# A raw weight tile of 6,208 instead of 6,152 bytes in a kernel bound by its matmuls

## The chip, the cores and the metric

The kernel runs on one core of a Trainium2 chip. The metric is the device time of one execution in microseconds (us); shorter is better. The engines are named as the profile names them: PE is TensorE (PEld its weight loads), DVE is VectorE, ACT is ScalarE, POOL is GpSimd, SP is SyncE, which issues most of the DMAs.

## The reference

Three stages, one behind the other, all in float32: attention with a soft cap on the scores, a gated MLP with an RMS norm ahead of it, and a second MLP with a PReLU.

```python
scores = cap * np.tanh(scale * (q @ k.T) / cap)        # 2 x 12 heads, 448 x 448, head_dim 64
attn   = softmax(scores); x = attn @ v                 # -> x: 896 tokens x 768
xn = x / rms(x) * rms_g
x  = (silu(xn @ w_gate) * (xn @ w_val)) @ w_out        # 768 -> 1536 -> 768
h  = x @ w_in                                          # 768 -> 2048
g  = np.maximum(h, 0) + alpha * np.minimum(h, 0)
out = g @ w_out2                                       # 2048 -> 768
```

## The kernel before

**Stages.** The attention works on 12 pairs of heads (6 pairs for each of 2 batches). All that follows, called the MLP part here, is a list of "slots": each slot is one product of 18 matmuls, and the work of the other engines is hung on slot numbers. The slots are the layers "g" (gate and value, 6 groups of 7 products), "o" (first output projection, 22 slots), "z" (4 groups of 7 products), and the last layer "c" and "f" (16 and 14 slots). The products of seven per group are a Strassen scheme (names P1 to P7, S1 to S4, T1 to T4).

**One matmul.** In the MLP part every matmul takes 128x128 weights (the stationary operand, 512 bytes in each partition) and 128x448 of activations (the moving operand, 1,792 bytes in each partition). Both are split in a high and a low half in the type fp32r, and one product is three sums of matmuls, high by high, low by high, high by low: 3 x 6 = 18 matmuls. Each matmul loads its own weights. The matmuls stand in lines 395 and 408 (layers g and z), 749 (layer o) and 775 (layers c and f). Five products have one of their matmuls cut in two (384 and 64 columns).

**Where the weights come from.** A DMA on SP's queue brings a unit of weights into a tile `raw` (line 101 and 102, three buffers, 8 bytes for each weight, landing two bytes behind the tile's start). ACT casts a part of it into `top` (line 113), DVE joins both into the float32 tile `wt` (line 118), DVE or POOL forms sums of such tiles (line 126), ACT rounds them into `wh` (line 133), and DVE subtracts to get `wl` (line 139). `wh` and `wl` are the weights of the matmuls. Two units of layer o, ("p", 0, 0) and ("p", 0, 1), are an exception: their halves are kept in tiles that otherwise hold activations (`w_kept`; the profile shows these weights as `xx` and `ks` in line 749). They serve the products c11 and c12. The products c21 and c22 of the same layer read the same activations as c11 and c12, with weights that lie in `wh` and `wl` as all others do.

**Addresses.** Tiles lie one behind the other in each partition of SBUF, pool by pool, each rounded up to 32 bytes. Constants, `wh` and `wl` lie ahead of `raw`; everything else lies behind it. The matmuls of the MLP part read slices at multiples of 512 bytes from the start of a weight tile and of 1,792 = 28 x 64 bytes from the start of an activation tile, so each operand has its tile's address modulo 64. The sums of the tile sizes give these starts:

| tile | start before | modulo 64 | start after | modulo 64 |
|---|---|---|---|---|
| `wh` (4 buffers), `wl` (4 buffers) | 8,480 to 29,984 | 32 | the same | 32 |
| `raw`, three buffers | 33,056; 39,232; 45,408 | 32; 0; 32 | 33,056; 39,264; 45,472 | 32; 32; 32 |
| `wt`, 10 buffers | from 51,584 | 0 | from 51,680 | 32 |
| activations of the MLP part, and the kept weights in them | from 82,304 | 0 | from 82,400 | 32 |
| attention: `hi`, `lo`, `vt`, `pt`, `ones`, `half`, `sel_t`, `r2` | from 150,496 | 32 | from 150,592 | 0 |

So before, a matmul of the MLP part has its weights at 32 and its moving operand at 0 modulo 64, but the matmuls of c11 and c12 have both at 0, and those of the attention both at 32.

Of the kernel before, what the change touches and what calls it, by code (L numbers as in the profile page):

```python
# [11 lines left out]
U16 = mybir.dt.uint16  # L12
# [5 lines left out]
P = 128  # L18
# [24 lines left out]
WT, WH, RAW = 10, 4, 3  # L43
# [14 lines left out]
def attn_moe_kernel(ctx: ExitStack, tc: tile.TileContext, units, qk_in, v, sel, w, gvec, alpha, out):  # L58
    nc = tc.nc
    const = ctx.enter_context(tc.tile_pool(name="const", bufs=1))  # L60
    wpool = ctx.enter_context(tc.tile_pool(name="w", bufs=1))
# [29 lines left out]
    UW = UK * P  # L91
    tops = [const.tile([P, UW], U32, name=f"top{i}") for i in range(2)]
    raw_t, f_t, h_t, l_t = {}, {}, {}, {}
# [4 lines left out]

    def w_load(u):
        i, n = units[u]  # L100
        raw_t[u] = wpool.tile([P, 4 * UW + 4], U16, tag="raw", name="raw", bufs=RAW)
        nc.sync.dma_start(out=raw_t[u][:, 1:4 * n + 1], in_=w[i][:, :n].bitcast(U16))

    def f_tile():
# [41 lines left out]
    def w_next(u):  # L146
        i = conv_seq.index(u) + RAW
        if i < len(conv_seq):
            w_load(conv_seq[i])
# [21 lines left out]
    hi, lo, raw, vt = {}, {}, {}, {}  # L171
# [242 lines left out]
    with tc.manual_schedule():  # L414
# [59 lines left out]
        for u in conv[:RAW]:  # L474
            z(0, w_load, u)
# [870 lines left out]
```

## Time and profile before

| | |
|---|---|
| time, median of 3 runs | 559.37 us (558.91 to 559.59) |
| the profiled execution's own time | 558.61 us |
| its span, from first to last instruction | 556.8 us |
| PE busy | 551.4 us, 99% |
| DVE, ACT, POOL busy | 446.9, 371.1, 97.7 us |
| granted TensorE clock | 1.00 of full speed |

The profiled execution is 1.8 us longer than its span and 0.76 us shorter than the median. A busy PE means that some matmul is in flight; since a matmul overlaps the next one, the time that one costs in a row of them is the distance from start to start, not its duration.

### The profile page before, as it was taken

The numbers are of one execution on the slowest core, as the hardware profiler recorded it, in microseconds if no ns is written. First come the engines' busy times: TensorE is split into PE (matmuls) and PEld (weight loads), VectorE is DVE, ScalarE is ACT, GpSimd is POOL, SyncE is SP. The second block draws the span as 40 slices with busy tenths as digits, with TensorE's granted clock in tenths as the row PEclk, the third lists the DMA queues.
The fourth block names the chain that finished last, engine by engine and source line by source line (L and its number), as shares of the span: only waits on it lengthen the run. The fifth ranks groups of instructions, "written<-read, shape, count | busy, mean of one in ns | idle before, by whom it ended". The sixth has DMA issues, their size and how long they took to land.

```text
span 556.8 us, 7691 instructions
## 1 busy us (share of the span) xinstructions
PE 551.4 (99%) x3061; PEld 461.0 (83%) x3061; DVE 446.9 (80%) x511; ACT 371.1 (67%) x433; POOL 97.7 (18%) x54
## 2 busy tenths in 40 slices
PE   8999999999999999999999999999999999999997
PEld 5544544799999999999999999999999999999996
DVE  4797888898998767878888798969866898999142
ACT  7989999568675455567755564787967996467110
POOL 0035762300254321010000048002111000000000
PEclk9999999999999999999999999999999999999999
DMA  7855420400434514065600662005512266013022
GB/s 255 281 182 189 145 76 4 171 1 1 167 117 154 171 74 169 13 214 181 213 4 1 227 236 104 1 0 171 186 42 85 87 226 227 0 58 114 0 100 99
DMA packets 17316, 66.09 MB, mean 119 GB/s; under 512 B 3584, under 2 KB 5504, under 8 KB 17280
## 3 DMA queue, kind: packets, MB, share of 16 engines
q1 hardware_dynamic: 16746, 65.08, 34.0%
q8 instruction: 24, 0.39, 0.3%
q10 hardware_dynamic: 390, 0.39, 0.2%
q0 software_dynamic: 144, 0.13, 0.1%
q14 instruction: 12, 0.10, 0.1%
HBM read 62.66 MB, written 2.75 MB: 117 GB/s over the span
## 4 chain that ended last, share of the span: by engine, by line
PE 97%; ACT 1%; DVE 1%; issue 0%; DVEq 0%
PE s L395 19%; PE x L395 13%; PE m L395 13%; PE s L775 9%; PE s L749 8%; PE x L775 7%; PE oo L236 6%; PE s L207 5%; PE x L749 4%; PE m L775 4%; PE rps L249 3%; PE m L749 2%; PE s L408 1%; PE x L408 1%; PE m L408 1%; ACT pt L221 1%
## 5 line engine op out<-in xcount | busy, mean ns | idle before, releaser
L133 ACT CAST wh<-wt 128x768 fp32r<-128x768 f32 x105 | 87.2, 833 | 68.2 <-PE s L775 24.6
L139 DVE TENSOR_TENSOR wl<-wt,wh 128x768 fp32r<-128x768 f32 x108 | 115.3, 1069 | 14.7 <-ACT wh L133 14.5
L126 POOL TENSOR_TENSOR wt<-wt 128x768 f32<-128x768 f32 x33 | 74.0, 2251 | 271.0 <-DVE wt L118 98.4
L113 ACT CAST top<-raw 128x768 f16<-128x768 bf16 x64 | 68.9, 1079 | 25.8 <-DVE wt L118 11.5
L118 DVE SCALAR_TENSOR_TENSOR wt<-raw,top 128x768 uint32<-128x768 uint32 x68 | 70.5, 1037 | 0.9 <-ACT top L113 0.9
L395 PE MATMUL s<-xx,wh 128*128 128x448 f32 x264 | 64.3, 368 | 0.0
L395 PEld LDWEIGHTS s<-xx,wh 128*128 128x128 f32 x264 | 49.5, 188 | 5.4 <-issue 0.7
L395 PE MATMUL x<-xx,wh 128*128 128x448 f32 x204 | 50.5, 369 | 0.0
L395 PE MATMUL m<-xx,wh 128*128 128x448 f32 x204 | 50.2, 368 | 0.0
L619 DVE TENSOR_TENSOR xx<-b,xx 128x896 fp32r<-128x896 f32 (+1 forms) x40 | 47.1, 1187 | 0.6 <-ACT xx L632 0.6
L216 ACT ACTIVATE pt<-s,cinv 128x896 f32<-128x896 f32 (+1 forms) x48 | 41.1, 911 | 5.6 <-PE s L207 5.2
L395 PEld LDWEIGHTS x<-xx,wh 128*128 128x128 f32 x204 | 38.2, 188 | 4.0 <-issue 0.4
L395 PEld LDWEIGHTS m<-xx,wh 128*128 128x128 f32 x204 | 38.3, 188 | 3.6
L775 PE MATMUL s<-xx,wh 128*128 128x448 f32 x132 | 40.7, 368 | 0.0
L236 PE MATMUL oo<-pt,vt 128*32 128x448 f32 x384 | 38.5, 540 | 0.4 <-ACT pt L221 0.3
L221 ACT ACTIVATE pt<-pt,cap_t 128x3136 f32<-128x3136 f32 (+2 forms) x13 | 35.3, 2713 | 0.4
L395 PE MATMUL s<-xx,wl 128*128 128x448 f32 x132 | 34.2, 367 | 0.0
L775 PE MATMUL x<-xx,wh 128*128 128x448 f32 x104 | 31.7, 367 | 0.0
L236 PEld LDWEIGHTS oo<-pt,vt 128*32 128x32 f32 x384 | 12.2, 110 | 23.6 <-issue 21.4
L749 PE MATMUL s<-xx,wh 128*128 128x448 f32 x96 | 27.5, 368 | 0.0
L775 PEld LDWEIGHTS s<-xx,wh 128*128 128x128 f32 x132 | 24.8, 188 | 2.3
L395 PEld LDWEIGHTS s<-xx,wl 128*128 128x128 f32 x132 | 24.8, 188 | 2.3
(223 smaller groups left out, 1119.5 us busy)
## 6 DMA issues: line engine op xcount, KB each, us to landing
raw<-w_in SPq DMA_DIRECT2D x68, 768.0 KB
rw<-qk_in SPq DMA_DIRECT2D x11, 480.0 KB
vt<-v_in SPq DMA_DIRECT2D x12, 256.0 KB
out<-b SPq DMA_DIRECT2D x2, 448.0 KB
out<-b SPq DMA_DIRECT2D x2, 224.0 KB
out<-e SPq DMA_DIRECT2D x1, 448.0 KB
out<-c SPq DMA_DIRECT2D x2, 224.0 KB
gt<-us SPq DMA_DIRECT2D x23, 3.5 KB
```

The costliest lines, as they stand in the source:

```text
L113: copy(top_of[u].bitcast(F16)[:, 1::2], raw_t[u].bitcast(BF16)[:, 4:4 * n + 4:4])
L118: nc.vector.scalar_tensor_tensor(out=f_t[u].bitcast(U32), in0=raw_t.pop(u).bitcast(U32)[:, 1:2 * n + 1:2], scalar=13, in1=top_of.pop(u), o ...
L126: add(out=t, in0=f_t[a], in1=f_t[b], op=op)
L133: copy(h_t[u], f_t[u].rearrange("p (k m) -> p k m", m=P))
L139: nc.vector.tensor_tensor(out=l_t[u], in0=f_t[u].rearrange("p (k m) -> p k m", m=P), in1=h_t[u], op=ALU.subtract)
L216: nc.scalar.activation(out=t[:, 2 * g:2 * g + w], in_=st.pop((i, g))[:, :w, :S], func=AF.Tanh, scale=cinv)
L221: nc.scalar.activation(out=t[:, done:to], in_=t[:, done:to], func=AF.Exp, scale=cap_t)
L236: nc.tensor.matmul(oo[i][q * Q:q * Q + Q, :S], vv[:, n, q % 2 * Q:q % 2 * Q + Q], t[:, min(n, TILES - 1), :], start=c == 0, stop=c == TG, ...
L395: nc.tensor.matmul(ps[:, r, c0:c1], lhs, rhs[:, c0:c1], start=first and n == 0, stop=n == len(mm) - 1, skip_group_check=True,)
L619: nc.vector.tensor_tensor(out=out, in0=a, in1=b, op=op)
L749: nc.tensor.matmul(dst[m], wt[:, kk * MB + m, :], x, start=first and u == 0 and kk == 0 and n == 0, stop=u == 1 and kk == 1 and n == 2, sk ...
L775: nc.tensor.matmul(dst[m], wt[:, kk * MB + m, :], x, start=start and ks + kk == 0 and i == 0, stop=fin and last and kk == 1 and i == 2, sk ...
```

## The change: 56 bytes more in each raw tile

The row of `raw` in the tile pool grows from 3,076 to 3,104 elements of two bytes. Nothing is written to or read from the added bytes. With the rounding to 32 bytes each of the three buffers takes 32 bytes more, so that all that lies behind `raw` moves up by 96 bytes, and its address modulo 64 by 32. The instructions and their order on every engine, the queues and the waits are the same.

```diff
     def w_load(u):
         i, n = units[u]
-        raw_t[u] = wpool.tile([P, 4 * UW + 4], U16, tag="raw", name="raw", bufs=RAW)
+        raw_t[u] = wpool.tile([P, 4 * UW + 32], U16, tag="raw", name="raw", bufs=RAW)
         nc.sync.dma_start(out=raw_t[u][:, 1:4 * n + 1], in_=w[i][:, :n].bitcast(U16))
```

## Rows read from the trace of the kernel before

**Rows 1.** The page, busy time: us (share of span) and instructions.

```profile
PE 551.4 (99%) x3061; PEld 461.0 (83%) x3061; DVE 446.9 (80%) x511; ACT 371.1 (67%) x433; POOL 97.7 (18%) x54
```

**Rows 2.** The waits of PE: engine, tile, line, cause: us, times, longest.

```profile
PE warm L419 <- DVE ones L416: 1.1, 1, 1.1
PE oo L236 <- ACT pt L221: 0.3, 1, 0.3
PE s L207 <- DVE eps_t L457: 0.2, 1, 0.2
```

**Rows 3.** The chain that ended last, in order of time: start us, us, what.

```profile
331.42 7.39 PE s L749 x36
...
342.50 3.70 PE m L395 x18
346.20 14.78 PE s L395 x72
360.98 3.70 PE x L395 x18
```

**Rows 4.** The timeline of PE around c11 and c12: start us, us, what.

```profile
264.90 0.57 PE L749 MATMUL s<-xx,wh 128*128 128x448 f32 x2
...
272.30 3.81 PE L749 MATMUL s<-xx 128*128 128x448 f32 x18
275.95 3.81 PE L749 MATMUL s<-xx,ks 128*128 128x448 f32 x18
279.60 0.57 PE L749 MATMUL x<-xx,wh 128*128 128x448 f32 x2
...
301.77 3.81 PE L749 MATMUL s<-xx 128*128 128x448 f32 x18
305.42 3.81 PE L749 MATMUL s<-xx,ks 128*128 128x448 f32 x18
309.08 0.57 PE L749 MATMUL s<-xx,wh 128*128 128x448 f32 x2
```

**Rows 5.** Busy time in four stretches of the MLP part.

```profile
core 0: us, PE busy (x) PEld busy (x) DVE busy (x) ACT busy (x) POOL busy (x), PEclk, DMA share, GB/s
264.90:272.30 7.40, 7.40 (x37) 6.76 (x36) 5.91 (x8) 6.17 (x9) 0.00 (x0) 1.00 0.69 248
272.30:279.60 7.30, 7.30 (x37) 6.76 (x36) 7.23 (x9) 5.52 (x8) 0.00 (x0) 1.00 0.45 145
301.77:309.08 7.31, 7.31 (x38) 6.76 (x37) 7.17 (x10) 3.40 (x4) 0.00 (x0) 1.00 0.13 27
346.20:360.98 14.78, 14.78 (x73) 13.51 (x73) 14.78 (x12) 11.54 (x14) 2.80 (x1) 1.00 0.00 1
```

**Rows 6.** Line 749 on PE: duration of one in ns, minimum/median/maximum.

```profile
L749 PE MATMUL s<-xx,wh x96: 365/368/370, 264.9 to 338.2; 128*128 128x448 f32 x96
L749 PE MATMUL s<-xx x36: 362/365/369, 272.3 to 305.2; 128*128 128x448 f32 x36
L749 PE MATMUL s<-xx,ks x36: 362/365/369, 275.9 to 308.9; 128*128 128x448 f32 x36
```

**Rows 7.** The timeline of PE in the scores of one attention pair.

```profile
40.64 0.37 PE L207 MATMUL s<-hi,lo 64*128 64x448 f32 x2
40.85 0.36 PE L207 MATMUL s<-lo,hi 64*128 64x448 f32 x2
...
41.85 0.38 PE L207 MATMUL s<-hi,lo 64*128 64x448 f32 x2
42.06 0.38 PE L207 MATMUL s<-lo,hi 64*128 64x448 f32 x2
```

**Rows 8.** PE alone in lines 395, 408, 749, 775, whole span: busy us (count).

```profile
0.00:556.80 556.80, 245.64 (x1193) 223.32 (x1193) 1.00 0.35 119
0.00:556.80 556.80, 14.95 (x72) 13.51 (x72) 1.00 0.35 119
0.00:556.80 556.80, 81.29 (x396) 74.33 (x396) 1.00 0.35 119
0.00:556.80 556.80, 111.04 (x540) 101.35 (x540) 1.00 0.35 119
```

**Rows 9.** DVE from 440 us on, by line: count, busy us, mean ns.

```profile
L139 DVE TENSOR_TENSOR wl<-wt,wh 128x768 fp32r<-128x768 f32 x21 | 19.9, 953 | 4.4 <-ACT wh L133 4.4
...
L126 DVE TENSOR_TENSOR wt<-wt 128x768 f32<-128x768 f32 x8 | 7.6, 952 | 0.0
```

**Rows 10.** The waits of ACT for weights' DMAs, whole span.

```profile
ACT top L113 <- DMA raw<-w_in: 9.5, 7, 2.5
```

**Rows 11.** The timeline of PE and ACT from 129.3 us on.

```profile
129.30 1.19 PE L408 MATMUL x<-xx,wh 128*128 128x448 f32 x5
130.33 1.40 PE L408 MATMUL m<-xx,wh 128*128 128x448 f32 x6
130.53 0.91 ACT L665 COPY b<-x 128x896 f32<-128x896 f32 x1 [2.50 <-PE x L408]
...
131.56 0.81 PE L395 MATMUL x<-xx,wh 128*128 128x448 f32 x3
...
134.08 0.92 ACT L665 COPY b<-m 128x896 f32<-128x896 f32 x1
...
135.28 0.78 PE L395 MATMUL m<-xx,wh 128*128 128x448 f32 x3
```

**Rows 12.** Busy time in the first third of the MLP part (columns as in rows 5).

```profile
98.00:131.00 33.00, 33.00 (x173) 28.29 (x166) 30.43 (x44) 18.89 (x28) 4.22 (x2) 1.00 0.20 73
131.00:257.50 126.50, 126.50 (x619) 115.61 (x618) 104.40 (x110) 80.59 (x104) 30.59 (x13) 1.00 0.38 132
```

## The prediction, made before the changed kernel ran

> **What bounds the kernel now.** I read the page's busy times first: PE is busy for 551.4 of 556.8 us, DVE for 80% and ACT for 67% [rows 1]. The reader is to see that no other engine comes near. The waits of PE come next: three in all, 1.6 us together, all in the warm-up and the attention [rows 2]. In the MLP part PE never waits. So the time there is the number of matmuls times the distance from one start to the next, and a change counts if it changes that distance. The distance is read from the chain: 72 matmuls in 14.78 us, 205.3 ns each [rows 3]. At the granted clock of 1.00, the level of 2.4 GHz [rows 5], 448 columns take 448 / 2.4 = 186.7 ns, so every matmul has 18.6 ns in which no column enters. The question is whether the change touches these 18.6 ns.
>
> **What the change does.** It adds, removes and reorders no instruction. It moves every address behind `raw` up by 32 modulo 64. I go through who reads these addresses.
>
> *The matmuls of the MLP part, without c11 and c12.* Lines 395, 408, 749 and 775 have 1193 + 72 + 396 + 540 = 2201 matmuls [rows 8], five products of them with one matmul cut in two, so 2196 whole ones. The kept weights serve 4 x 18 = 72 [rows 4]; 2124 are left. Each has its weights at 32 and its moving operand at 0 modulo 64 now, and both at 32 after. The trace of before has no matmul of this kind with both at 32, but it has the 72, with both at 0. In the timeline the four slots of c11 and c12 take 279.60 - 272.30 = 7.30 us and 309.08 - 301.77 = 7.31 us for 36 matmuls each [rows 4]: 14.61 / 72 = 202.9 ns. The 36 ahead of c11, in the same line, take 272.30 - 264.90 = 7.40 us, 205.6 ns; and c22, which reads the very activations that c12 reads, takes 7.39 us for 36, 205.3 ns [rows 3]. The durations say the same in another way: 362/365/369 ns at c11 and c12, 365/368/370 ns at the others of the line [rows 6]. Only the weights' place is different, so that place is worth 205.3 - 202.9 = 2.4 ns by the starts and 3 ns by the median durations.
>
> Is it the other engines? Between 272.30 and 279.60 us DVE is busier than before it (7.23 of 7.30 us against 5.91 of 7.40) and DMAs less busy (0.45 against 0.69); between 346.20 and 360.98 us DMAs do nothing and DVE is busy throughout, and the matmuls still take 205.3 ns [rows 3, 5]. So neither explains the 2.4 ns.
>
> Is it that both lie at 0, or that both lie at the same place? The attention has both at 32. In the steady part of one pair's scores, seven steps (each two matmuls on 64 rows that run side by side) take 42.06 - 40.64 = 1.42 us, 202.9 ns a step [rows 7]. These are matmuls of half the rows, so they are weaker evidence, but they fall on the value of c11 and c12 and not on 205.3. In the attention `lo` and `hi` differ by 64 modulo 128 (their tiles start 15,424 bytes apart, 120.5 x 128), and the steps with one of each are in these seven, so a difference of 64 does no harm either; after the change weights and moving operands of the MLP part differ by just that, modulo 128.
>
> The saving of one matmul is therefore bounded by 0 (the relation is not the cause) and 3.0 ns (the durations). I take 2.5 ns, near the difference of the starts: 2124 x 2.5 ns = 5.3 us. The end with 3.0 ns gives 6.4 us.
>
> A rule of the Trainium skill speaks against this. In the rows, the place of the weights alone changes the distance between matmuls by 2.4 ns [rows 3, 4]. The page "TensorE: Matmul & The Clock Gate" (section "Step-by-step: what each phase is for") says that PE reads moving operand and weights through two independent ports, so that a weight load takes no read bandwidth from the matmul that runs. By that rule two operands could not be in each other's way at any addresses, and the sum would be 0, 559.4 us; by the rows it is 5.3 us. I go by the rows.
>
> *c11 and c12, and the attention.* Both operands move by 32 together: c11 and c12 from both at 0 to both at 32, the attention the other way. By the reasoning above, neither changes: 0 us. If a start at 32 cost each of the 72 a loss of 2.5 ns, that would be 0.2 us.
>
> *DVE, ACT and POOL.* `wl` is made from operands at 0 and 32 in 953 ns, and a sum of `wt` tiles of the same size, all at 0, takes 952 ns [rows 9]. So a mix of places costs DVE nothing, and all operands at 32 should not either. I take 0.
>
> *The DMAs into `raw`.* The second of three buffers moves from 0 to 32, where the first and third are already. ACT waits for such DMAs 7 times, 9.5 us in all [rows 10], and PE waits for nothing in the MLP part, so the slack of ACT covers it. 0 us.
>
> *What a faster PE runs into.* If PE saves 1.2% in the MLP part, work that is not paced by PE comes later relative to it. The closest places: at 131.56 us PE starts into a bank that an ACT copy has freed at 130.53 + 0.91 = 131.44 us, 0.12 us before; at 135.28 us into one that was freed at 135.00 us, 0.28 us before [rows 11]. The first copy itself waited for PE's matmuls (2.50 us idle, ended by PE), and only six matmuls of line 408 lie between: PE gains 6 x 2.5 = 15 ns against it. For the second, some 23 matmuls lie between 130.53 and 135.28 us: 58 ns. Both covers hold. I take 0 and keep 0.3 us as the price if some such places do not hold.
>
> Sum: -5.3 us. The profiled execution would go from 558.61 to 553.3 us; its span from 556.8 to 551.5 us. It was 0.76 us below the median, so the median goes from 559.37 to **554.0 us** (559.37 - 5.3, rounded down, since one bound is 3.0 ns).
>
> **The rivals.** *The place itself counts, not the relation (slower).* The 72 of c11 and c12 are also the only matmuls with both operands at a multiple of 64, where a weight row fills 8 blocks of 64 bytes and a moving row 28; at 32 they touch 9 and 29. If each operand that starts at 32 costs 2.5 ns, then 2124 matmuls have one such operand now and two afterwards, and 72 none now and two afterwards: 2124 x 2.5 + 72 x 5.0 ns = 5.7 us more, 565.0 us. For it: c11 and c12 can't tell it from my reading. Against it: the steps of the attention, with both at 32, take 202.9 ns and not 208 [rows 7]. It would decide the sign as soon as a moving operand at 32 costs more than the relation saves. Chance 0.05.
>
> *Another property of the kept weights (no change).* They lie above byte 82,400 as the activations do, while `wh` and `wl` lie below 33,056; so do weights and moving operands of the attention lie together. If nearness or the region counts, the change does nothing: 559.4 us. Against it, only that distances within the slow group vary widely (`wh` buffers 3,072 bytes apart, activations from 82,304 to above 200,000) with the same 3.70 us for each 18 matmuls [rows 3]. The Trainium skill's rule of the two ports gives the same time. Chance 0.10.
>
> *The waits take a part.* DVE or ACT can't follow in the first third of the MLP part, where DVE is busy for 30.43 of 33.0 and 104.40 of 126.5 us [rows 12]. If all that PE gains there is lost (173 + 619, some 790 matmuls, 790 x 2.5 = 2.0 us), 556.0 us is left. Chance 0.05.
>
> **How the numbers follow.** My forecast, 5.3 us saved in full, has a chance of 0.80; its own range is 553.0 us (3.0 ns each, 6.4 us saved) to 555.1 us (2.0 ns each, 4.2 us saved). The case in which waits take a part reaches to 556.5 us; with it the range holds 0.85, less what misses at its edges. Runs of before differ by 0.7 us, and 0.2% (1.1 us) is about what a measurement of this kernel can tell from no change. Faster by more than that: 0.80 + 0.05 = 0.85; within it: 0.10; slower: 0.05.
>
> **What the profile of the changed kernel would show.** In the chain, 18 matmuls of line 395 or 775 in 3.65 us in place of 3.70; in line 749 a median duration of 365 ns in all groups, no longer in `xx` and `ks` alone; c11 and c12 still 7.30 us for 36, and the attention still as long as it was. PE's waits still the three. DVE's line 139 still at 953 ns. I am wrong if the matmuls stay at 205.3 ns (nearness, or the two ports), if they go to 208 ns and c11 and c12 with them (the place itself), or if they go to 202.9 ns and PE shows new waits in the MLP part.

## The result: faster by 1.2%, more than forecast

The changed kernel takes 552.50 us (median of 4 runs, 552.27 to 552.85); the kernel before, 559.19 us (558.91 to 559.59) in the same comparison. The ratio is 0.988, with a 95% interval of 0.9863 to 0.9898: 6.7 us saved. I had forecast 5.3 us and 554.0 us, with a range from 553.0 to 556.5 us; the time lies 0.5 us below that range.

The chain of the changed kernel that ended last, in order of time (start us, us, what), over the stretch of [rows 3]:

```profile
339.86 3.64 PE m L395 x18
343.50 14.56 PE s L395 x72
358.06 3.64 PE x L395 x18
```

72 matmuls take 14.56 us in place of 14.78: 202.2 ns from start to start in place of 205.3. That is 3.06 ns saved for each of 2124 matmuls, 6.5 us. The four lines of matmuls show the same. PE's busy time in lines 395, 408, 749 and 775 over the whole span (the columns of [rows 8]):

```profile
0.00:551.10 551.10, 242.02 (x1193) 223.06 (x1193) 1.00 0.36 120
0.00:551.10 551.10, 14.72 (x72) 13.50 (x72) 1.00 0.36 120
0.00:551.10 551.10, 80.27 (x396) 74.26 (x396) 1.00 0.36 120
0.00:551.10 551.10, 109.36 (x540) 101.23 (x540) 1.00 0.36 120
```

Together they are 446.37 us, where [rows 8] have 452.92: 6.55 us less. The weight loads' time (the third number with its count) has hardly moved: it is the distance between matmuls that shrank, not the loads.

c11 and c12, whose weights lie among the activations, are as they were. The timeline of PE there (as [rows 4]):

```profile
270.52 3.81 PE L749 MATMUL s<-xx 128*128 128x448 f32 x18
274.17 3.81 PE L749 MATMUL s<-xx,ks 128*128 128x448 f32 x18
277.81 0.57 PE L749 MATMUL x<-xx,wh 128*128 128x448 f32 x2
```

36 matmuls in 277.81 - 270.52 = 7.29 us, 202.5 ns, against 7.30 us in [rows 4]. So the others have not come up to these 72; at 202.2 ns they have gone just past them.

PE's waits, and DVE from 434 us on (the rows that answer to [rows 2, 9]):

```profile
PE warm L419 <- DVE ones L416: 1.1, 1, 1.1
PE oo L236 <- ACT pt L221: 0.3, 1, 0.3
PE rps L322 <- DVE us L272: 0.2, 1, 0.2
PE s L207 <- ACT hi L444: 0.2, 1, 0.2
```

```profile
L139 DVE TENSOR_TENSOR wl<-wt,wh 128x768 fp32r<-128x768 f32 x21 | 19.9, 953 | 3.2 <-ACT wh L133 3.1
...
L126 DVE TENSOR_TENSOR wt<-wt 128x768 f32<-128x768 f32 x8 | 7.6, 952 | 0.0
```

No wait is in the MLP part, and DVE takes 953 and 952 ns, as before. The profiled execution saved a little less than the 6.55 us, 558.61 - 552.85 = 5.76 us, because its attention was longer: the MLP part begins 0.74 us later. Its chain begins with the first load, which the chain of before does not hold, and PE waited once more for DVE in the attention (the third wait above). The chain at the start and at the first matmul of line 395:

```profile
0.74 3.18 DMA rw<-qk_in
3.94 0.57 ACT hi L444
4.56 2.72 PE s L207 x12
...
100.71 2.43 PE s L395 x11
```

In the kernel before, the first matmul of line 395 stands at 99.97 us in the same view. The first experiment speaks against the addresses as the cause: its attention lies at 0 modulo 64 too, and its MLP part begins at 99.99 us.

### The profile page after: what moved, and what is told of

It reads as the page before. It is cut to its first block, busy times and chain, and to the rows that moved or that the text cites. A ratio compares the mean times of both kernels' runs of the same rounds, so it can differ in the third digit from the quotient of the medians.

```text
span 551.1 us, 7691 instructions
## 1 busy us (share of the span) xinstructions
PE 545.6 (99%) x3061; PEld 461.3 (84%) x3061; DVE 448.5 (81%) x511; ACT 370.6 (67%) x433; POOL 98.8 (18%) x54
## 4 chain that ended last, share of the span: by engine, by line
PE 96%; DVE 1%; ACT 1%; DMA 1%; issue 0%; DVEq 0%
PE s L395 19%; PE x L395 13%; PE m L395 13%; PE s L775 9%; PE s L749 8%; PE x L775 7%; PE oo L236 6%; PE s L207 5%; PE x L749 4%; PE m L775 4%; PE rps L249 3%; PE m L749 2%; PE s L408 1%; PE m L408 1%; PE x L408 1%; ACT pt L221 1%
## 5 line engine op out<-in xcount | busy, mean ns | idle before, releaser
L139 DVE TENSOR_TENSOR wl<-wt,wh 128x768 fp32r<-128x768 f32 x108 | 113.6, 1053 | 12.5 <-ACT wh L133 12.2
L113 ACT CAST top<-raw 128x768 f16<-128x768 bf16 x64 | 68.8, 1076 | 27.0 <-DMA raw<-w_in 11.7
L395 PE MATMUL s<-xx,wh 128*128 128x448 f32 x264 | 63.5, 364 | 0.0
L619 DVE TENSOR_TENSOR xx<-b,xx 128x896 fp32r<-128x896 f32 (+1 forms) x40 | 48.8, 1228 | 0.6 <-ACT xx L632 0.6
L775 PE MATMUL s<-xx,wh 128*128 128x448 f32 x132 | 40.0, 362 | 0.0
L395 PE MATMUL s<-xx,wl 128*128 128x448 f32 x132 | 33.8, 364 | 0.0
L749 PE MATMUL s<-xx,wh 128*128 128x448 f32 x96 | 27.2, 364 | 0.0
L775 PE MATMUL s<-xx,wl 128*128 128x448 f32 x72 | 26.5, 367 | 0.0
```

Source lines behind the costliest of these rows:

```text
L113: copy(top_of[u].bitcast(F16)[:, 1::2], raw_t[u].bitcast(BF16)[:, 4:4 * n + 4:4])
L139: nc.vector.tensor_tensor(out=l_t[u], in0=f_t[u].rearrange("p (k m) -> p k m", m=P), in1=h_t[u], op=ALU.subtract)
L395: nc.tensor.matmul(ps[:, r, c0:c1], lhs, rhs[:, c0:c1], start=first and n == 0, stop=n == len(mm) - 1, skip_group_check=True,)
L619: nc.vector.tensor_tensor(out=out, in0=a, in1=b, op=op)
L749: nc.tensor.matmul(dst[m], wt[:, kk * MB + m, :], x, start=first and u == 0 and kk == 0 and n == 0, stop=u == 1 and kk == 1 and n == 2, sk ...
L775: nc.tensor.matmul(dst[m], wt[:, kk * MB + m, :], x, start=start and ks + kk == 0 and i == 0, stop=fin and last and kk == 1 and i == 2, sk ...
```

## The experiments

My theory was that equality modulo 64 of the two addresses counts. The rivals were each operand's own start, some other property of the place, and (after the result) a finer relation. In what follows "the distance" is the moving operand's address minus the weights' address, modulo 256; it is the same for all matmuls of the MLP part except those of c11 and c12, where it is 0 in every kernel (one kernel, the mix, has two distances). Before, it is 96; in the changed kernel, 192.

**Four shifts.** Unused bytes are put behind `raw`, or ahead of the weights, in the kernel before. The diff shows both edits with 16 elements of two bytes, that is 32 bytes; 64 bytes are 32 elements. The first two kernels have the first edit, the third has both, the fourth has the second alone:

```diff
+    pad = []
+
     def f_tile():
+        if not pad:
+            pad.append(wpool.tile([P, 16], U16, tag="pad", name="pad", bufs=1))
         return wpool.tile([P, UW], F32, tag="wt", name="wt", bufs=WT)
...
+    lead = const.tile([P, 16], U16, name="lead")
     tops = [const.tile([P, UW], U32, name=f"top{i}") for i in range(2)]
```

32 bytes behind `raw` (distance 128):

> The raw tile as before (6,152 bytes), and 32 unused bytes behind the three raw buffers: everything behind moves up by 32 in place of 96. Weights and moving operands of the MLP part both at 32 modulo 64, and now equal modulo 128 as well (in the changed kernel they differ by 64 modulo 128). The raw buffers stay where they were. If the relation modulo 64 is the cause: 202.2 ns a matmul as in the changed kernel, about 552.5 us. If the relation modulo 128 has a part in it: 202.85 ns, the value of c11 and c12 before, about 554 us. If the place of the raw buffers (the DMAs' landing address) is the cause: 205.3 ns, 559.2 us.

64 bytes behind `raw` (distance 160):

> The same with 64 unused bytes: moving operands at 0 modulo 64 again, weights at 32; the attention at 32 as before. If the relation modulo 64 is the cause: 205.3 ns, 559.2 us, as before. If a finer relation counts (difference of 32 modulo 128 here, 96 before), another value than 205.3 ns. If any shift of the tiles behind raw is the cause (by their region or by what lies next to what): faster than before, near 552.5 us.

32 bytes ahead of the weights and 32 behind `raw` (distance 128):

> 32 unused bytes ahead of the weight tiles and 32 behind raw: weights and moving operands of the MLP part all at 0 modulo 64, equal modulo 128. If the relation alone counts: the same as with 32 bytes behind raw alone (both at 32), 552.5 to 554 us. If an operand's own start counts, it is faster than that: each operand at 0 saves up to 2.5 ns more, 197 to 200 ns a matmul, 543 to 549 us.

32 bytes ahead of the weights (distance 96):

> 32 unused bytes ahead of the weight tiles: weights go to 0 and moving operands to 32 modulo 64, the two places of before exchanged. If the relation counts: 205.3 ns, 559.2 us, no change. If only the weights' start counts: 202.9 ns or less, 553 to 554 us. If only the moving operand's start counts: 208 ns, 565 us.

Measured against the kernel before (558.82 us): 556.58 us (ratio 0.9959, interval 0.9944 to 0.9974), 547.88 us (0.9819, 0.9788 to 0.9850), 556.30 us (0.9954, 0.9940 to 0.9969) and 558.95 us (1.0004, 0.9994 to 1.0013). Of the second, one execution took 551.51 us and the other three 547.60 to 548.11 us; the trace is of one of the three, and why the one was longer is open. The 72 matmuls of [rows 3] in the chains of the four, in this order (the lines are those of each kernel; it is line 395 of the kernel before):

```profile
344.95 14.69 PE s L399 x72
```

```profile
340.55 14.40 PE s L399 x72
```

```profile
345.01 14.69 PE s L400 x72
```

```profile
346.58 14.78 PE s L396 x72
```

My theory fell with the second: its operands lie at 32 and 0 modulo 64, as before, and at 14.40 / 72 = 200.0 ns it beats the changed kernel by 2.2 ns a matmul. The first has equal addresses modulo 64 and got 204.0 ns, less than half of the gain. But the third and fourth show that the relation counts and not the place. With both operands at 0 it is the same 14.69 us as with both at 32; with the two places exchanged it is the same 14.78 us as before. In both pairs weights and moving operands have moved by 32 bytes together, and the pace is unchanged.

**The other half of the circle.** Small constant tiles, moved from ahead of the weights to a place behind all weight tiles, change the distance by 128 and 160:

```diff
     wpool = ctx.enter_context(tc.tile_pool(name="w", bufs=1))
+    mid = ctx.enter_context(tc.tile_pool(name="mid", bufs=1))
     xpool = ctx.enter_context(tc.tile_pool(name="x", bufs=1))
...
-    cap_t = const.tile([P, 1], F32, name="cap_t")
-    tiny = const.tile([P, 1], F32, name="tiny")
+    cap_t = mid.tile([P, 1], F32, name="cap_t")
+    tiny = mid.tile([P, 1], F32, name="tiny")
     cinv = aconst.tile([P, 1], F32, name="cinv")
     g_t = const.tile([P, KD], F32, name="g_t")
-    al_t = const.tile([P, K2N], F32, name="al_t")
+    al_t = mid.tile([P, K2N], F32, name="al_t")
```

That is distance 224; with `g_t` moved as well it is 0, and with 32 or 64 bytes behind `raw` on top, 32 or 64.

> Moving operand minus weights is 224 modulo 256 (three small constant tiles now lie between the weights and the activations, so that the weights move down by 128; the rest stays). If the distance counts modulo 128, this is the case of before (96): 205.3 ns, 559 us. If it counts modulo 256 or more, another value. My first theory, the relation modulo 64 alone, says 205.3 ns as well, but it is refuted already by the run with 64 bytes behind raw.

> The distance is 0 modulo 256 (all four small constant tiles between). Modulo 128 the same as with 32 bytes behind raw: 204.0 ns, 556.5 us. If it counts modulo 256: the distance of c11 and c12 with their kept weights, 202.5 to 206.4 ns, 553 to 561 us.

> The distance is 32 modulo 256. Modulo 128 the same as with 64 bytes behind raw, the fastest so far: 200.1 ns, 548 us. If it counts modulo 256, another value.

> The distance is 64 modulo 256. Modulo 128 the same as in the changed kernel: 202.2 ns, 552.5 us. If it counts modulo 256, another value.

Measured against 558.99 us: 556.12 us (ratio 0.9950, interval 0.9935 to 0.9965), 553.22 us (0.9901, 0.9885 to 0.9918), 561.71 us (1.0047, 1.0032 to 1.0062) and 548.25 us (0.9809, 0.9794 to 0.9823). The same 72 matmuls in the chain:

```profile
345.12 14.72 PE s L395 x72
```

```profile
343.42 14.59 PE s L395 x72
```

```profile
347.23 14.88 PE s L395 x72
```

```profile
341.31 14.40 PE s L395 x72
```

A period of 128 is refuted: 32 is the slowest of all, while 160 is among the fastest. All eight distances, each as the time of these 72 matmuls divided by 72:

| distance modulo 256 | kernel | from start to start, these 72 | time |
|---|---|---|---|
| 0 | constants moved | 202.6 ns | 553.22 us |
| 32 | constants moved, 32 behind | 206.7 ns | 561.71 us |
| 64 | constants moved, 64 behind | 200.0 ns | 548.25 us |
| 96 | before | 205.3 ns | 558.7 to 559.2 us |
| 128 | 32 behind | 204.0 ns | 556.58 us |
| 160 | 64 behind | 200.0 ns | 547.88 us |
| 192 | the changed kernel | 202.2 ns | 552.50 us |
| 224 | three constants moved | 204.4 ns | 556.12 us |

The distances that are multiples of 64 (0, 64, 128, 192) are faster in the mean, 202.2 ns against 204.1, but the place in the circle counts as much.

The distance does not fix the pace alone. Two of these kernels change their pace on the way, with weights in `wh` and `wl` as ever and at one distance. The chain of distance 224:

```profile
227.56 3.68 PE s L395 x18
...
242.28 3.76 PE m L395 x19
246.04 3.66 PE s L395 x18
```

Here 18 matmuls go from 3.68 us (204.4 ns) to 3.66 (203.3 ns) behind a product with one matmul cut in two (the x19), one of the five that every kernel has. They are back at 3.68 us behind c11, and from the next such product, at 396.64 us, to the end they take 3.66 again. In the kernel of distance 32, 18 matmuls take 3.68 us (204.4 ns) between 135 and 176 us in place of 3.72. So the table gives the pace of one stretch, and the times of these two kernels are mixtures.

Whether a distance beyond 256 counts is not settled. The slices of the activations are 1,792 = 7 x 256 bytes apart and those of the weights 512, so that the distance modulo 512 takes both values within every group of 18, and the sums of the groups can't tell. By the single starts in line 395, the middle one of each three, which is the one 256 bytes off, takes 205.4 ns before, and the others 205.3; with 64 bytes behind `raw` all take 200.1. But in the changed kernel the three take 202.9, 200.2 and 203.6 ns; its starts also repeat in threes (below), so the two can't be told apart there.

**A mix, and the best distance at no cost.** If each matmul had a price by its own pair of addresses, `wh` at 160 and `wl` at 96 would give two thirds of the gain. The edit is a tile of 64 bytes between the two:

```diff
...
+                h_t["g", g, x] = wpool.tile([P, UK, P], F32R, tag="wh", name="wh", bufs=WH)
+                gap = gap or wpool.tile([P, 32], U16, tag="gap", name="gap", bufs=1)
+                l_t["g", g, x] = wpool.tile([P, UK, P], F32R, tag="wl", name="wl", bufs=WH)
```

> 64 unused bytes between the wh and the wl tiles: the distance modulo 256 is 160 for wh (200.1 ns where all weights had it) and 96 for wl (205.3 ns, as before). If each matmul's distance from start to start is set by its own pair of addresses: two thirds at 200.1 and one third at 205.3 ns, 201.8 ns in the mean, 551.8 us. If it is set by the weights that are loaded meanwhile, the same mean, but the long ones stand one matmul earlier (3rd to 5th of nine in line 395, in place of 4th to 6th). If the rhythm is one for the whole run of matmuls (c11 and c12 took two values at one and the same pair of addresses), a single value between or at one end: 548 to 559 us, and no difference by position.

In the other kernel only `cap_t` and `tiny` move behind `raw`, as in the diff of the second group, which makes the distance 160 without an added byte:

> The best distance, 160 modulo 256, without a byte more: two constant tiles of 32 bytes move from ahead of the weights to behind raw, so that the weights and raw lie 64 bytes lower and everything else where it was before. If the distance between weights and moving operands alone counts: 200.1 ns and 548 us, as with 64 bytes behind raw. If 64 bytes behind raw helped for another reason (the attention's place, the raw tiles' place against the rest): near 559 us.

Measured against 558.66 us: 557.98 us (ratio 0.9991, interval 0.9982 to 1.0001) for the mix and 548.22 us (0.9808, 0.9794 to 0.9823) for the moved constants. Their 72 matmuls:

```profile
345.78 14.77 PE s L395 x72
```

```profile
340.47 14.40 PE s L395 x72
```

The second confirms the distance once more: in this kernel the activations and the tiles of the attention lie where they lay before, the weight tiles lie 64 bytes lower, and the gain is that of 64 bytes behind `raw`. The first refutes a price for each matmul by its own addresses: 205.1 ns in place of 201.8. By the starts in its trace, a matmul of line 395 that stands between two others of distance 160 takes 206.3 ns (mean of 525), the very addresses that take 200.0 ns when `wl` lies at 160 too. My third case, one rhythm without a difference by position, wasn't right either: a `wl` matmul between two others of `wl` takes 202.6 ns (mean of 127).

**The rhythm.** c11 and c12 always have distance 0, but with 32 bytes behind `raw` they take 7.43 us for 36 matmuls, 206.4 ns, where before they took 7.30. Both operands have moved by 32 bytes together, and with 32 bytes ahead of the weights, where c11 and c12 lie at the same places, they take 7.30 us. So what differs is the pace of what runs ahead of them. That what runs ahead can decide is seen within one execution, that of distance 64, where c11 takes 276.10 - 268.81 = 7.29 us and c12 305.14 - 297.70 = 7.44:

```profile
268.81 3.81 PE L749 MATMUL s<-xx 128*128 128x448 f32 x18
272.46 3.80 PE L749 MATMUL s<-xx,ks 128*128 128x448 f32 x18
276.10 0.56 PE L749 MATMUL x<-xx,wh 128*128 128x448 f32 x2
...
297.70 3.88 PE L749 MATMUL s<-xx 128*128 128x448 f32 x18
301.42 3.88 PE L749 MATMUL s<-xx,ks 128*128 128x448 f32 x18
305.14 0.57 PE L749 MATMUL s<-xx,wh 128*128 128x448 f32 x2
```

To test it I cut one matmul, the first of c11, in the kernel with 32 bytes behind `raw`, into 384 and 64 or into 224 and 224 columns:

```diff
-                        nc.tensor.matmul(
-                            dst[m], wt[:, kk * MB + m, :], x, start=first and u == 0 and kk == 0 and n == 0,
+                        for cs in (slice(0, 384), slice(384, S)) if (p, u, kk, m, n) == ("c11", 0, 0, 0, 0) else (slice(0, S),):
+                            nc.tensor.matmul(
+                                dst[m][:, cs], wt[:, kk * MB + m, :], x[:, cs], start=first and u == 0 and kk == 0 and n == 0,
...
```

> The kernel with 32 bytes behind raw (distance 128), where c11 and c12 both ran at 206.4 ns, with one difference: the first matmul of c11 is cut in two, 384 and 64 columns. All addresses are the same. If the distance from start to start is a matter of addresses and of their order alone, c11 stays at 206.4 ns (7.43 us for 36, plus some 0.03 to 0.2 us for the cut). If it is a rhythm that a run of equal matmuls keeps once it has fallen into it, the cut can throw c11 out of it, to the other value seen for these addresses, 202.7 ns (7.30 us for 36 plus the cut); c12, which isn't cut, stays at 206.4 ns.

> The same with the cut in the middle (224 and 224 columns), which disturbs at another point. Addresses alone: c11 stays at 206.4 ns. A rhythm: c11 can change to 202.7 ns, or stay if this cut happens to keep the phase; c12 stays at 206.4 ns.

One execution each: 555.82 and 556.36 us, beside 558.82 us for the kernel before. The timeline of PE at c11 and c12, first without the cut, then with 384 and 64:

```profile
271.19 3.88 PE L753 MATMUL s<-xx 128*128 128x448 f32 x18
274.90 3.88 PE L753 MATMUL s<-xx,ks 128*128 128x448 f32 x18
278.62 0.57 PE L753 MATMUL x<-xx,wh 128*128 128x448 f32 x2
...
300.65 3.88 PE L753 MATMUL s<-xx 128*128 128x448 f32 x18
304.36 3.88 PE L753 MATMUL s<-xx,ks 128*128 128x448 f32 x18
308.08 0.57 PE L753 MATMUL s<-xx,wh 128*128 128x448 f32 x2
```

```profile
274.85 3.81 PE L749 MATMUL s<-xx,ks 128*128 128x448 f32 x18
278.49 0.57 PE L749 MATMUL x<-xx,wh 128*128 128x448 f32 x2
...
300.51 3.81 PE L749 MATMUL s<-xx 128*128 128x448 f32 x18
304.16 3.81 PE L749 MATMUL s<-xx,ks 128*128 128x448 f32 x18
307.81 0.57 PE L749 MATMUL s<-xx,wh 128*128 128x448 f32 x2
```

Without the cut, the 18 of the second unit take 278.62 - 274.90 = 3.72 us; with it, 278.49 - 274.85 = 3.64 us. So c11 fell from one rhythm into the other at unchanged addresses. And c12, 22 us later and not cut, went with it: 307.81 - 300.51 = 7.30 us against 7.43. There I was wrong: if the cut did that too, its effect was carried through all the matmuls of distance 128 in between. The cut in the middle changed nothing: 7.43 us for c12 and 3.71 us for the second unit of c11:

```profile
275.20 3.88 PE L749 MATMUL s<-xx,ks 128*128 128x448 f32 x18
278.91 0.57 PE L749 MATMUL x<-xx,wh 128*128 128x448 f32 x2
...
300.94 3.88 PE L749 MATMUL s<-xx 128*128 128x448 f32 x18
304.66 3.88 PE L749 MATMUL s<-xx,ks 128*128 128x448 f32 x18
308.37 0.57 PE L749 MATMUL s<-xx,wh 128*128 128x448 f32 x2
```

Each of these kernels was traced in one execution, so the two cuts alone do not exclude a chance difference between executions; with the changes of pace within one execution, above, history is the likelier reading. The single starts show that most of these paces are means of a repeating pattern. In the 72 of the chain, the matmuls with 32 bytes behind `raw` repeat some 212, 200, 209, 196 and 203 ns, five that do not fit the nine of a row of a product; those of the changed kernel repeat some 199, 201 and 207; those of distance 160 take 200 ns each.

So distance and history both go with the pace. Why stays open; no row shows PE's reads of its operands.

## Why the prediction was right in sign and too small

*What bounds the kernel: right.* PE waits for nothing in the MLP part, before and after, and the saving of the four lines, 6.55 us, is nearly that of the kernel, 6.7 us.

*The saving of one matmul: the step that failed.* I put it at 2.5 ns, with 3.0 as its upper bound; it measured 3.06 by the chain, 2124 x 3.06 = 6.5 us. The sum is otherwise as I made it. Of the 0.5 us below the range, 0.1 us is what 3.06 ns give beyond 3.0, and 0.2 us is the median of before, 559.19 in place of 559.37 us; the rest is less than the 0.6 us by which the runs of the changed kernel differ. The size came from c11 and c12 as stand-ins for what all matmuls would be, because both have equal addresses modulo 64. But they stand for distance 0, and the change makes it 192. When all matmuls were brought to distance 0, they took 202.6 ns, near the 202.9 of c11 and c12, and the time was 553.22 us. So the stand-in gave about the price of the distance that it had, and that by luck too, since c11 and c12 take 202.8 or 206.4 ns at one distance. I had seen that modulo 128 the two would differ, and argued from the attention that 64 there "does no harm"; it does 0.4 ns of good, and the bound taken from the stand-ins' durations did not cover it. No row of before could give a bound for distance 192; the runs went down to 200.0 ns, 5.3 ns below the kernel before.

*The reason: half right.* That the relation of the two addresses and not the place counts is shown (both at 0 is as both at 32, and an exchange of the places is no change). That equality modulo 64 is the cause is refuted: at distance 160, one of the two fastest, the operands differ by 32 modulo 64. Another shift that makes the addresses equal modulo 64, 32 bytes behind `raw`, is worth 558.82 - 556.58 = 2.2 us in place of 6.7. So the size was luck, and the sign in part: of the seven other distances, all but 32 are faster than the 96 of before, so that almost any shift would have had the sign that I forecast.

*c11, c12 and the attention unchanged: right here.* 7.29 us against 7.30; in the longer attention of the profiled execution the chain begins with a load, and the first experiment does not show the delay. That c11 and c12 can't change was wrong in general: they took 7.43 us with 32 bytes behind `raw`, at a distance of 0 as ever.

*DVE 0, the DMAs 0, the waits 0: right.* 953 ns as before. ACT waits 11.7 us for the weights' DMAs in place of 9.5 [rows 10], which PE does not feel. PE has four waits where I forecast three, but the new one, 0.2 us, is in the attention and none is in the MLP part.

*The rivals.* The place itself (565.0 us) and the region or nearness (559.4 us) are refuted by the result and by the four shifts, and no share of the gain was lost to waits. The Trainium skill, page "TensorE: Matmul & The Clock Gate", section "Step-by-step: what each phase is for", gives PE two independent ports to read its two operands, so that a weight load takes no read bandwidth from the running matmul. The time that I took from this rule, 559.4 us, did not come: the pace goes from 200.0 to 206.7 ns with the distance of the two addresses. Whether it is the reads that meet is not shown.

## What to carry to other kernels

Where PE is busy throughout and every matmul loads its own weights, as here, try shifts of 32 bytes between weights and moving operands round a whole circle of 256 bytes, and read the distance from start to start for each. Here it was worth 1.9% (547.88 and 548.22 us against 558.82 and 558.66 us), and two constant tiles moved to another pool gave it at no memory; the first shift that helps need not be the best, and the kernel before had the second slowest of eight. A small group of instructions that differs in one property is a good witness that something counts, but a witness of its own value of it only, and of the run of instructions around it.

## What was not expected of the hardware

One and the same matmul, 128x128 weights and 448 columns at a granted clock of 1.00, came 200.0 to 206.7 ns after the one before it, depending on the distance of its operands modulo 256. A run of equal matmuls can hold either of two paces at one distance: 202.8 and 206.4 ns in c11 and c12, 204.4 and 203.3 ns at distance 224. With one matmul cut in two, two runs 22 us apart had the other pace than in the kernel without the cut (one execution of each).
